# Six row-tile buffers for five, convolution stores and loads moved behind a countdown, and a paired inverse moved by two slots

## The chip, the cores and the metric

The kernel runs on one core of a Trainium2 chip. The metric is the device time of one execution in microseconds. Before the change the median of three runs is 1872.39 us (1871.93 to 1872.93).

## What is computed

The reference is the forward pass and all gradients of a layer with two branches on a layer norm of `A_q` (2048 rows of 1024). Branch A multiplies a long causal convolution, done by a Fourier transform of length 4096 per column, with the row; branch B is a gated MLP of width 3584. Cut to what matters:

```python
xn = _layernorm(x)                                     # x = A_q
# branch A
k_shift = sum(k_pad[:, t:t + S] * shift_k[:, ks - 1 - t] for t in range(ks))   # ks = 4
kv = k_shift * v
y = irfft2(rfft2(kv_pad) * rfft2(ssm_k_pad).T)[:S] + kv * ssm_D
a = xn * y
# branch B
gate, up = xn @ W_gate, xn @ W_up
gate = gate * (gate > 0)
b = (gate * up) @ W_down
out = x + a + b                                        # and the vjp of it for grad_out
```

The outputs are `out` and the gradients of `A_q`, `A_k`, `A_v`, `A_shift_k`, `A_ssm_k`, `A_ssm_D` and the three weights. All are bfloat16.

## The kernel before, in words

**Two branches on one TensorE.** Class `LnMlp` holds branch B's large products, class `ABranch` the convolution and its gradient. B's phases are generators that yield at the end of each piece of work with a number of nanoseconds. The main loop takes that number off a budget, and whenever the budget is used up it takes one *slot* of A: `ABranch.steps` (L577) runs through `slots` (L677) for eight groups of 128 columns. A slot has a tensor part `p` (a few small matmuls into PSUM tiles `ps_c`, evicted by ScalarE) and a vector part `d` (one VectorE step). It charges 1900 ns, or, once B is past its hidden phase (`dense`), 1250 ns when it has no tensor part.

**B's phases.** `hidden` (L1100) walks 14 blocks: seven column blocks of 512 for each half of the rows, eight row tiles a block. A row tile takes three products of eight 128x512 matmuls: `gate` (tile `ps_g`), `up` (`ps_u`) and `grad_row` (`ps_h`), all issued at L1041. ScalarE writes the ReLU of the gate into the row tile `ru` (L1149), VectorE the masked `up` (L1156) and their product `ht` (L1162); ScalarE copies `ps_h` to `gh` (L1284), and VectorE multiplies `ru` by it (L1285). `ht` is stored to `h_d` (L1167), `ru` to `ug_d` (L1290), both two ticks after they are asked for (`defer`, `tick`). `ru` comes from the pool `e2` (five buffers, L839; the later phases take their output tiles `wo` and `wi` from it), `ht` and `gh` from `e1`. The last four rows of a block are taken in another order, gate gate up gate gate up grad up up grad grad grad (`last_rows`); from there to the block's end `hold` is set. At the end of the last block, and before the next phase, `g_nat`, the natural rows of `grad_out`, are loaded into tiles that were `xnT` and `goT`.

`grad_down` computes the gradient of `W_down`, `grad_in` those of `W_gate` and `W_up`, in products of sixteen matmuls over the row tiles (`gemm16`, L1376). The first and the last turn of the former and the first of the latter are done by `four` (L1392): four PSUM banks at a time, so that the row tiles are needed more slowly, or come free sooner; meanwhile `cap` is 2 instead of 3, so a slot of A takes at most two pairs of banks. `xn_nat` rows take the tiles of `g_nat` when the last `four` of `grad_down` is done with them. Then follow `out_phase` (L1540) and `grad_x` (L1672), for which A's memory is released: weights `wd` (L1501) and the transposed row tiles `hT` (L1506) go there.

**PSUM.** One pool of eight banks, `b_ps`, serves both branches. A's slot takes up to six of them.

**A's transfers.** Everything is issued on SP's queue: A's loads (L99), A's stores (L107), B's loads, slabs (L1358) and stores. While `strict` is set, each engine's instructions stay in program order, so what SP waits for holds up all that is behind it. Stores are issued where the code calls `store` (L105). Loads are put into `queue` by `fetch` and `later`; after each slot `steps` issues one of them (L609) unless `hold` is set, and `need` (L262) issues those that are about to be read, hold or no hold. `load_filter` issues the first half of the filter rows `hn` and puts the second, `load_rest`, at the end of the queue. Most of A's tiles have one buffer, so a load waits until the tile's last reader is done.

**A's time-domain tiles.** `ttile` (L256) gives tiles of 19 rows x 128 from three tags: `gkv` and `gk` in tag ts0, `gks` and `gh` in ts1, `gv` and `yt` in ts2. Rows 16 to 18 hold the halo of `gks`.

**The paired inverse.** `inv_a_pair` gives four jobs `inv[0..3]`; `inv[1]` reads spectra that the complex product `cmul(H, K, ...)` has just written, and is the tensor part of the slot right behind `halo` (L747). `tables` (L140) fills the sine tables before the first slot.

Of the kernel before, what the change touches and what calls it, by code (L numbers as in the profile page):

```python
# [11 lines left out]
BF16 = mybir.dt.bfloat16  # L12
F32 = mybir.dt.float32
I32 = mybir.dt.int32
# [3 lines left out]
P = 128  # L18
# [27 lines left out]
NB1 = 32  # L46


class ABranch:
# [5 lines left out]
    def __init__(self, tc, pri, S, D, k, v, g, shift_k, ssm_k, ssm_D, xn_d, y_d, sk_d, gks_d, gh_d, out_gk,  # L55
                 out_gv, out_gsD):
        assert S == 2048 and D % P == 0
        self.tc, self.nc, self.pri = tc, tc.nc, pri
        self.S, self.D, self.NG = S, D, D // P
        self.k, self.v, self.g, self.shift_k, self.ssm_k, self.ssm_D = k, v, g, shift_k, ssm_k, ssm_D  # L60
        self.xn_d, self.y_d, self.sk_d = xn_d, y_d, sk_d
        self.gks_d, self.gh_d, self.out_gk, self.out_gv, self.out_gsD = gks_d, gh_d, out_gk, out_gv, out_gsD
        self.pools, self.pin, self.dense, self.queue = [], False, False, []
        self.cap = 3

    def pool(self, name, bufs, **kw):
        p = self.tc.alloc_tile_pool(name=name, bufs=bufs, **kw)
# [35 lines left out]
            self.pri.pin(ins)  # L103

    def store(self, out, in_):  # L105
        self.pri.late()
        self.pri.pin(self.nc.sync.dma_start(out=out, in_=in_))  # L107

    def open(self):
        R = "right"  # L110
# [29 lines left out]
    def tables(self):  # L140
        nc, con, big, pri = self.nc, self.con, self.big, self.pri
# [40 lines left out]
        for ri in range(2):  # L182
            off = lin(b32, -1024.0, 1024.0 * (1 + ri) + 2048.0, "offF%d" % ri)
            q = big.tile([P, NB1, NB1], I32, name="qF", tag="big")
# [20 lines left out]
        q = big.tile([P, 3, 8, NB1], I32, name="qI", tag="big")  # L205
# [7 lines left out]

        kk = lin(b5, 4.0, 1.0, "kkB")
        ob = lin(b32, 32.0, 96.0, "obB")
        itB = con.tile([P, NB1], I32, name="itB")
        hold(nc.gpsimd.iota(itB[:], pattern=[[1, NB1]], base=0, channel_multiplier=0))
        V.tensor_scalar(out=itB[:], in0=itB[:], scalar1=kk[:], scalar2=ob[:], op0=ALU.mult, op1=ALU.add)
        V.tensor_single_scalar(out=itB[:], in_=itB[:], scalar=127, op=ALU.bitwise_and)
        trB = con.tile([P, NB1], F32, name="trB")  # L220
        nc.scalar.activation(out=trB[:], in_=itB[:], func=ACT.Sin, scale=TWO_PI / 128, bias=negpi[:])
        for h in range(2):
            m = lin(b64, (2 * h - 1) / 1024.0, (1 - h) / 1024.0, "mB%d" % h)
# [30 lines left out]
    HOME = dict(gkv=0, gks=1, gv=2, gk=0, yt=2, gh=1)  # L254

    def ttile(self, name):  # L256
        return self.ts.tile([P, 19, P], BF16, name=name, tag="ts%d" % self.HOME[name])

    def later(self, f, st):
        self.queue.append((f, st))  # L260

    def need(self, f, st):  # L262

        while (f, st) in self.queue:
            self.issue()

    def issue(self):
        f, st = self.queue.pop(0)
        f(st)

    def load_filter(self, st):
        hn = self.lng.tile([P, 19, P], BF16, name="hn", tag="hk")[:, 0:16, :].rearrange("p r c -> p (r c)")
        st["hn"] = hn.rearrange("p (h c n) -> p h c n", h=2, n=NB1)
        self.load_rows(st, 0)
        self.later(self.load_rest, st)

    def load_rows(self, st, h):
        hv = self.ssm_k[st["cg"]].rearrange("(h x c) (q n) -> x h q c n", h=2, x=2, n=NB1)
# [298 lines left out]
    def steps(self):  # L577

        sk_t = self.shift_rows()
        self.pin = True
        yield 10000
        self.load(self.sk_d, sk_t[:])
        yield 25000
        self.sts = [dict(gi=gi, cg=slice(gi * P, (gi + 1) * P)) for gi in range(self.NG)]
        st = self.sts[0]
        self.load_filter(st)
        self.issue()
        yield 3400  # L590
        self.load_g(st)
        yield 3400
        self.load_v(st)
        yield 3400
        self.load_taps(st)
        yield 6800
        self.load_xn(st)
        self.pin = False
        self.pri.strict = True
        self.open_arena()  # L600
        for st in self.sts:
            for p, d in self.slots(st, st["gi"]):
                *more, last = self.parts(p)
                for fs in more:
                    self.tensor(fs)
                    yield self.DENSE[0]
                self.tensor(last)
                self.run(d)
                if self.queue and not self.hold():  # L609
                    self.issue()  # L610
                yield self.DENSE[p is None] if self.dense else self.SLOT

    def begin(self, st):
        st["ksh"] = self.lng.tile([P, 16, P], BF16, name="ksh")
# [62 lines left out]
    def slots(self, st, gi):  # L677
# [68 lines left out]
        yield [], lambda: self.halo(st)  # L746
        ia, inv = self.inv_a_pair()  # L747
        q = self.cmul(K, G, True, G, 1)
        yield inv[1], q
        for _ in range(4):  # L750
            yield None, q
        q = self.cmul(H, K, False, K, 1)
        cross, gk = [inv[0], None], None
        if not last:
# [71 lines left out]
class LnMlp:  # L826
# [7 lines left out]
    def open_left(self):  # L834
        tc = self.tc
        self.per = tc.alloc_tile_pool(name="b_per", bufs=1, side="left")
        self.actp = tc.alloc_tile_pool(name="b_act", bufs=1, side="left")
        self.w2 = tc.alloc_tile_pool(name="b_w2", bufs=1, side="left")
        self.e2 = tc.alloc_tile_pool(name="b_e2", bufs=5, side="left")  # L839
        self.e1 = tc.alloc_tile_pool(name="b_e1", bufs=5, side="left")  # L840
        self.ps = tc.alloc_tile_pool(name="b_ps", bufs=8, space=bass.MemoryType.PSUM)
        self.ln_x, self.xn, self.todo, self.hold = [], [], [[]], False
        self.rstd = self.per.tile([P, self.ST], F32, name="rstd")
        self.ident = self.per.tile([P, P], BF16, name="ident")
        make_identity(self.nc, self.ident[:])
# [859 lines left out]
@with_exitstack  # L1705
def kernel(
    ctx: ExitStack,
    tc: tile.TileContext,
    A_q: bass.AP,
    A_k: bass.AP,  # L1710
    A_v: bass.AP,
    A_shift_k: bass.AP,
    A_ssm_k: bass.AP,
    A_ssm_D: bass.AP,
    B_x: bass.AP,
    B_W_gate: bass.AP,
    B_W_up: bass.AP,
    B_W_down: bass.AP,
    grad_out: bass.AP,
    out_0: bass.AP,  # L1720
    out_1: bass.AP,
    out_2: bass.AP,
    out_3: bass.AP,
    out_4: bass.AP,
    out_5: bass.AP,
    out_6: bass.AP,
    out_7: bass.AP,
    out_8: bass.AP,
    out_9: bass.AP,
):  # L1730
    _, S, D = A_q.shape
    F = B_W_gate.shape[1]
    assert S % 256 == 0 and D == 1024 and F % 256 == 0
    x, g = A_q[0], grad_out[0]
    dram = ctx.enter_context(tc.tile_pool(name="dram", bufs=1, space=bass.MemoryType.DRAM))
    xn_d = dram.tile([S, D], BF16, name="xn_d")
    y_d = dram.tile([S, D], BF16, name="y_d")
    h_d = dram.tile([S, F], BF16, name="h_d")
    ug_d = dram.tile([S, 2, F], BF16, name="ug_d")

    gks_d = dram.tile([D // P, P, S], BF16, name="gks_d")
    gh_d = dram.tile([D // P, P, S], BF16, name="gh_d")
    sk_d = dram.tile([D // P * 4, P], BF16, name="sk_d")

    pri = Pri(tc)
    b = LnMlp(tc, pri, S, D, F)
    a = ABranch(tc, pri, S, D, A_k[0], A_v[0], g, A_shift_k, A_ssm_k, A_ssm_D, xn_d, y_d, sk_d[:], gks_d, gh_d, out_2[0],
                out_3[0], out_6)
    b.open_left()
    a.open()  # L1750
    a.identA, a.bank, b.branch = b.ident, b.ps_tile, a
    a.hold = lambda: b.hold
    pri.now()
    load = lambda i: b.ln_load(x, a.lnx, i)
    load(0)
    load(1)
    b.first_root()
    first = [b.col_block(B_W_gate, 0, "wg", 0)]
    first.append(b.col_block(B_W_up, 0, "wu", 1, lambda: load(2)))
    load(3)  # L1760
    first.append(b.row_block_T(B_W_down, 0, "wdT", 2, lambda: load(4)))
    goT = [b.load_T(g, i, "goT", 8 + i) for i in range(2)]
    load(5)
    goT += [b.load_T(g, i, "goT", 8 + i) for i in range(2, 4)]
    a.load_shift()
    ln = b.layer_norm(xn_d, a.tmp, "tmp", a.sm)
    def mlp():
        yield False, b.hidden(first, goT, load, ln, a.tables, B_W_gate, B_W_up, B_W_down, g, xn_d, h_d, ug_d)
        yield True, b.grad_down(xn_d, ug_d, h_d, out_9)
        yield True, b.grad_in(ug_d, out_7, out_8)  # L1770

    a_steps, left = a.steps(), A_START
    if True:
        for a.dense, phase in mlp():
            for ns in phase:
                left -= ns
                while a_steps is not None and left <= 0:
                    d = next(a_steps, None)
                    if d is None:
                        a.close()  # L1780
                        a_steps = None
                        pri.strict = False
                        b.open_right(B_W_down)
                    else:
                        left += d
    b.close_left()
    b.out_phase(x, xn_d, y_d, h_d, B_W_gate, B_W_up, out_0[0])
    b.grad_x(x, g, xn_d, y_d, h_d, ug_d, B_W_down, out_0[0], out_1[0],
             (A_k[0], gks_d, gh_d, out_4, out_5))
# [30 lines left out]
```

## Time and profile before

| what | us |
|---|---|
| median of three runs | 1872.39 |
| the profiled execution | 1871.87 |
| its span, first to last instruction | 1869.7 |
| TensorE busy / idle | 1853.3 / 16.4 |
| VectorE, ScalarE, POOL busy | 1113.7, 646.3, 19.4 |
| mean granted TensorE clock | 0.998 |

In the waits by engine, ScalarE's ReLU at L1149 waits for `ug_d<-ru`, the store of a row tile, five times, 19.5 us in all and 8.0 at most. SP's longest wait for A is that of a store at L107 for ScalarE's `yt`, 9.8 us; its loads at L99 wait 30.6 us in nine places for `ps_c` matmuls. The moved instructions of A in the table of DMA issues: `hn` 32 issues of 128 KB, 4.7 us median to landing; `vt`, `xt`, `kp` 16 each of 256 KB, 4.1 to 4.3 us; `gv`, `yt`, `gk` 16 each of 256 KB, 6.7, 4.5 and 5.0 us; `gks` and `gh` eight each of 512 KB, 2.7 and 7.2 us.

How to read it: TensorE's busy time is nearly the whole span, so a part matters if it ends an idle stretch of TensorE, or makes one. An idle stretch shows as a number ahead of a group or of a piece of the timeline, with the instruction or DMA that ended it. The granted clock of a window is a share of full speed. On SP's timeline "SPq" lines are issues: start, time the issue took, line, what is moved.

### The profile page before, as it was taken

What the parts mean: (1) busy time and instruction counts of PE and PEld (TensorE: products, weight loads), DVE (VectorE), ACT (ScalarE), POOL (GpSimd) and SP (SyncE); (2) the same over time, 40 slices, a digit from 0 to 9 for tenths busy, and PEclk for the clock granted to TensorE, in tenths of its full rate; (3) what the DMA queues carried; (4) which work ended last, traced back from release to release, by engine and by line L of the source; (5) the groups of instructions that cost most, each with busy time, mean ns of one, the idle gap of its engine ahead of it and who ended that gap; (6) DMA issues with size and microseconds to landing.
All of it is one profiled execution on the core that took longest, in us unless ns stands there. A gap on an engine that the chain in (4) does not pass through costs nothing.

```text
span 1869.7 us, 32060 instructions
## 1 busy us (share of the span) xinstructions
PE 1853.3 (99%) x13061; PEld 846.7 (45%) x13061; DVE 1113.7 (60%) x1635; ACT 646.3 (35%) x1215; POOL 19.4 (1%) x51
## 2 busy tenths in 40 slices
PE   9999999899999999999999999999999999999999
PEld 4444444444444444444444444444444544444444
DVE  6656897697789668485785677720222222466652
ACT  5744445445444454544545554331000000111100
POOL 1000000000000000000000000000000000000000
PEclk9999999999999999999999999999999999999999
DMA  9897678868868767467556454469999857799973
GB/s 265 244 224 183 151 199 202 213 163 185 188 151 204 216 160 189 125 168 205 164 144 160 118 161 118 144 178 274 261 215 257 206 135 174 179 210 203 209 154 74
DMA packets 748132, 344.65 MB, mean 184 GB/s; under 512 B 576088, under 2 KB 715344, under 8 KB 747984
## 3 DMA queue, kind: packets, MB, share of 16 engines
q1 hardware_dynamic: 736848, 320.31, 71.0%
q10 hardware_dynamic: 9504, 17.04, 3.0%
q0 software_dynamic: 1632, 5.24, 0.8%
q8 instruction: 102, 1.67, 0.4%
q14 instruction: 46, 0.38, 0.1%
HBM read 143.79 MB, written 103.83 MB: 132 GB/s over the span
## 4 chain that ended last, share of the span: by engine, by line
PE 95%; DVE 2%; DMA 2%; ACT 1%; issue 0%; SPq 0%; ACTq 0%; DVEq 0%
PE ps_x L1672 21%; PE ps_w L1376 20%; PE ps_o L1540 10%; PE ps_g L1041 10%; PE ps_u L1041 10%; PE ps_h L1041 9%; PE ps_d L1376 9%; PE ps_c L83 4%; PE ps_d L1392 1%; DVE ru L1156 0%; DMA g_nat<-in_grad_out_dram 0%; DVE arena L334 0%; PE ps_r L1574 0%; PE ps_w L1392 0%; DMA xn_nat<-xn_d 0%
## 5 line engine op out<-in xcount | busy, mean ns | idle before, releaser
L1376 PE MATMUL ps_w<-ugs,xn_nat 128*128 128x512 bf16 x1728 | 381.3, 379 | 0.0
L87 ACT CAST arena<-ps_c 128x512 bf16<-128x512 f32 x576 | 293.9, 610 | 109.2 <-PE ps_c L83 108.9
L1041 PEld LDWEIGHTS <-xnT 128*128 128x128 bf16 x1792 | 172.5, 98 | 215.7 <-issue 12.6
L334 DVE STREAM_TRANSPOSE arena<-arena 128x1024 f32<-128x1024 f32 x96 | 179.5, 1931 | 137.0 <-ACT arena L87 118.0
L1376 PEld LDWEIGHTS <-xn_nat 128*128 128x128 bf16 x1728 | 165.3, 98 | 201.4 <-issue 7.3
L1041 PE MATMUL ps_g<-wg,xnT 128*128 128x512 bf16 x896 | 206.5, 381 | 5.6 <-ACT ru L1149 4.9
L1041 PE MATMUL ps_u<-wu,xnT 128*128 128x512 bf16 x896 | 206.0, 379 | 0.0
L1041 PE MATMUL ps_h<-wdT,goT 128*128 128x512 bf16 x896 | 204.8, 379 | 0.0
L1672 PE MATMUL ps_x<-wgT,ggT 128*128 128x512 bf16 x896 | 198.6, 379 | 0.0
L1672 PE MATMUL ps_x<-wuT,guT 128*128 128x512 bf16 x896 | 198.6, 379 | 0.0
L1690 ACT ACTIVATE w<-xn,m 128x512 f32<-128x512 bf16 x32 | 24.4, 808 | 480.3 <-DVE m L1683 366.7
L1540 PE MATMUL ps_o<-wd,hT 128*128 128x512 bf16 (+1 forms) x896 | 187.6, 372 | 0.0
L1376 PE MATMUL ps_d<-g_nat,hs 128*128 128x512 bf16 x768 | 170.1, 379 | 0.0
L1672 PEld LDWEIGHTS <-guT 128*128 128x128 bf16 x896 | 87.7, 98 | 105.7
L1672 PEld LDWEIGHTS <-ggT 128*128 128x128 bf16 x896 | 87.7, 98 | 105.5
L1041 PEld LDWEIGHTS <-goT 128*128 128x128 bf16 x896 | 86.0, 98 | 103.9 <-issue 2.9
L1540 PEld LDWEIGHTS <-hT 128*128 128x128 bf16 x896 | 87.7, 98 | 99.9
L1284 ACT CAST gh<-ps_h 128x512 bf16<-128x512 f32 x112 | 66.5, 595 | 178.3 <-PE ps_h L1041 177.2
L1379 ACT CAST wi<-ps_w 128x512 bf16<-128x512 f32 x108 | 64.6, 598 | 181.5 <-PE ps_w L1376 145.2
L1156 DVE SCALAR_TENSOR_TENSOR ru<-ru,ps_u 128x512 bf16<-128x512 bf16 x112 | 76.5, 683 | 81.6 <-PE ps_u L1041 56.0
L1532 DVE TENSOR_TENSOR ya<-ya,xe 128x1024 bf16<-128x1024 bf16 x16 | 11.1, 692 | 173.6 <-DMA xe<-xn_d 173.6
L91 DVE TENSOR_TENSOR t<-arena 128x2048 bf16<-128x2048 bf16 x96 | 113.9, 1219 | 0.4
(145 smaller groups left out, 1393.6 us busy)
## 6 DMA issues: line engine op xcount, KB each, us to landing
ugs<-ug_d SPq DMA_DIRECT2D x112, 256.0 KB, 5.0
ug_d<-ru SPq DMA_DIRECT2D x110, 256.0 KB, 3.0
wg<-in_B_W_gate_dram SPq DMA_DIRECT2D x56, 256.0 KB, 3.6
wu<-in_B_W_up_dram SPq DMA_DIRECT2D x56, 256.0 KB, 3.2
hs<-h_d SPq DMA_DIRECT2D x56, 256.0 KB, 4.2
out_dram<-wi SPq DMA_DIRECT2D x56, 256.0 KB, 2.5
h_d<-ht SPq DMA_DIRECT2D x108, 128.0 KB, 3.3
gt<-in_grad_out_dram SPq DMA_DIRECT2D x32, 256.0 KB, 4.5
```

The lines of the kernel that those rows point to most:

```text
L83: self.pri.pin(self.nc.tensor.matmul(out, lhsT=lhsT, rhs=rhs, start=start, stop=stop))
L87: self.pri.pin(self.nc.scalar.copy(out=out, in_=in_))
L91: self.pri.pin(self.nc.vector.tensor_tensor(out=out, in0=in0, in1=in1, op=op))
L334: self.pri.pin(self.nc.vector.transpose(out=df[:, c0:c0 + 32, :], in_=sf[:, c0:c0 + 32, :]))
L1041: self.pri.pin(self.nc.tensor.matmul(ps[:], lhsT=xT[:, kt * P:(kt + 1) * P], rhs=w(kt), start=(kt == 0), stop=(kt == self.DT - 1)), always ...
L1156: return self.pri.pin(nc.vector.scalar_tensor_tensor(out=ru[s][:, 1, :], in0=ru[s][:, 0, :], scalar=0.0, in1=ps[:], op0=ALU.is_gt, op1=ALU ...
L1284: self.pri.pin(nc.scalar.copy(out=gh[:], in_=ps[:]))
L1376: self.pri.pin(self.nc.tensor.matmul(ps[:], lhsT=lhsT(st), rhs=rhs(st), start=(st == 0), stop=(st == self.ST - 1)))
L1379: self.pri.pin(self.nc.scalar.copy(out=out, in_=ps[:]))
L1540: nc.tensor.matmul(ps, lhsT=hT[:, kt, :], rhs=self.wd[:, kt, oc], start=(kt == 0), stop=(kt == self.FT - 1))
L1672: nc.tensor.matmul(ps, lhsT=T[:, kt, :], rhs=W[:, kt, oc], start=(i == 0), stop=(i == n - 1))
L1690: nc.scalar.activation(out=w[:, oc], in_=xn[:, oc], func=ACT.Identity, scale=m[:, 7:8], bias=m[:, 6:7])
```

## The change

It does six things.

- The pool `e2` has six buffers instead of five.
- `store` no longer issues: it puts the transfer in a list `out` with a countdown of 3. After each slot's vector part `stores` takes one off every countdown and issues, in order, those at 0. A store thus goes out at the end of the third slot from where it was called. At A's end the rest is issued.
- `later` gives each queued load the same countdown; the queue's first is issued when it has reached 0. The countdown runs on in the slot that would have issued the load, so it goes out two slots after that at the earliest. `load_rest` goes to the front of the queue without a countdown.
- `a.hold` is also true while `cap` is 2, that is during `four`. `need` overrides both.
- `inv[1]` stands in the third of its five slots instead of the first; the number of slots is the same.
- `ttile` gives 16 rows unless the tag is ts1, and two small tiles of the sine tables, `itB` and `trB`, take the buffers of tags ts2 and ts1.

```diff
-        self.cap = 3
+        self.cap, self.out = 3, []
...
     def store(self, out, in_):
-        self.pri.late()
-        self.pri.pin(self.nc.sync.dma_start(out=out, in_=in_))
+        self.out.append([self.WAIT, out, in_])
+
+    def stores(self):
+        for o in self.out:
+            o[0] -= 1
+        while self.out and self.out[0][0] <= 0:
+            _, out, in_ = self.out.pop(0)
+            self.pri.late()
+            self.pri.pin(self.nc.sync.dma_start(out=out, in_=in_))
+
+    WAIT = 3
...
-        itB = con.tile([P, NB1], I32, name="itB")
+        itB = self.ts.tile([P, NB1], I32, name="itB", tag="ts2")
...
-        trB = con.tile([P, NB1], F32, name="trB")
+        trB = self.ts.tile([P, NB1], F32, name="trB", tag="ts1")
...
     def ttile(self, name):
-        return self.ts.tile([P, 19, P], BF16, name=name, tag="ts%d" % self.HOME[name])
+        h = self.HOME[name]
+        return self.ts.tile([P, 19 if h == 1 else 16, P], BF16, name=name, tag="ts%d" % h)
 
     def later(self, f, st):
-        self.queue.append((f, st))
+        self.queue.append([f, st, self.WAIT])
 
     def need(self, f, st):
 
-        while (f, st) in self.queue:
+        while any(e[0] == f and e[1] is st for e in self.queue):
             self.issue()
 
     def issue(self):
-        f, st = self.queue.pop(0)
+        f, st, _ = self.queue.pop(0)
         f(st)
...
         self.load_rows(st, 0)
-        self.later(self.load_rest, st)
+        self.queue.insert(0, [self.load_rest, st, 0])
...
                 self.run(d)
-                if self.queue and not self.hold():
+                self.stores()
+                for e in self.queue:
+                    e[2] -= 1
+                if self.queue and self.queue[0][2] <= 0 and not self.hold():
                     self.issue()
                 yield self.DENSE[p is None] if self.dense else self.SLOT
+        while self.out:
+            self.stores()
...
         q = self.cmul(K, G, True, G, 1)
+        yield None, q
+        yield None, q
         yield inv[1], q
-        for _ in range(4):
-            yield None, q
+        yield None, q
+        yield None, q
...
-        self.e2 = tc.alloc_tile_pool(name="b_e2", bufs=5, side="left")
+        self.e2 = tc.alloc_tile_pool(name="b_e2", bufs=6, side="left")
...
-    a.hold = lambda: b.hold
+    a.hold = lambda: b.hold or a.cap == 2
```

## The prediction

> **What bounds the kernel now.** I read the page's busy times first, then TensorE's groups by shape with the idle time ahead of them, then windows and timelines around the largest gaps.
>
> ```profile
> PE 1853.3 (99%) x13061; PEld 846.7 (45%) x13061; DVE 1113.7 (60%) x1635; ACT 646.3 (35%) x1215; POOL 19.4 (1%) x51
> ```
> TensorE works 1853.3 of 1869.7 us. No matmul is added or removed, so nothing can be won but the 16.4 us of idle time and what a lowered clock costs. The groups say who ended the idle time:
>
> ```profile
> L1041 PE MATMUL ps_g<-wg,xnT 128*128 128x512 bf16 x896 | 206.5, 381 | 5.6 <-ACT ru L1149 4.9 <-DVE xnT L1085 0.3 <-DVE ru L1156 0.2
> L1392 PE MATMUL ps_d<-g_nat,hs 128*128 128x512 bf16 x128 | 30.6, 391 | 1.8 <-DMA g_nat<-in_grad_out_dram 1.8
> L83 PE MATMUL ps_c<-arena,IA 32*64 32x256 bf16 x1024 | 30.0, 274 | 1.2 <-DVE arena L91 1.2
> L1392 PE MATMUL ps_w<-ugs,xn_nat 128*128 128x512 bf16 x64 | 15.0, 380 | 0.7 <-DMA xn_nat<-xn_d 0.7
> ```
> That is 5.6 + 1.8 + 1.2 + 0.7 = 9.3 us; the rest is the start (3.7 with 0.3 of ps_g's), the tail after the last matmul (3.2) and one wait of the convolution for ScalarE (0.7). The clock dips at the first two places:
>
> ```profile
> 345.00:350.00 5.00, 2.88 (x58) 1.39 (x57) 1.11 (x2) 0.00 (x0) 0.00 (x0) 1.00 0.87 241
> 350.00:355.00 5.00, 2.20 (x6) 0.83 (x6) 1.22 (x3) 2.85 (x6) 0.00 (x0) 0.74 1.03 289
> 355.00:360.00 5.00, 5.00 (x52) 2.15 (x51) 0.76 (x1) 3.35 (x8) 0.00 (x0) 0.92 0.95 247
> ...
> 650.00:655.00 5.00, 3.71 (x17) 1.04 (x17) 0.95 (x1) 2.35 (x5) 0.00 (x0) 0.78 1.02 337
> 655.00:660.00 5.00, 5.00 (x22) 2.11 (x21) 5.00 (x4) 1.33 (x3) 0.00 (x0) 0.88 0.99 218
> ```
> Column three from the end is the granted clock: (0.26 + 0.08) x 5 = 1.7 us lost at 350, (0.22 + 0.12) x 5 = 1.7 at 650.
>
> **The 4.9 us stall at 347.9.** The PE, ScalarE and SP timelines:
>
> ```profile
> 345.98 1.90 PE L1041 MATMUL ps_u<-wu,xnT 128*128 128x512 bf16 x8
> 352.80 5.08 PE L1041 MATMUL ps_g<-wg,xnT 128*128 128x512 bf16 x16 [4.92 <-ACT ru L1149]
> ```
> ```profile
> 343.58 0.60 ACT L1149 ACTIVATE ru<-ps_g 128x512 bf16<-128x512 f32 x1 [0.33 <-PE ps_g L1041]
> 352.15 0.60 ACT L1149 ACTIVATE ru<-ps_g 128x512 bf16<-128x512 f32 x1 [7.97 <-DMA ug_d<-ru]
> ```
> ```profile
> 339.07 1.47 SPq L1290 DMA_DIRECT2D ug_d<-ru  x1
> 340.59 2.17 SPq L99 DMA_DIRECT2D hn<-in_A_ssm_k_dram  x2
> 342.86 2.00 SPq L107 DMA_DIRECT2D out_dram<-gk  x2
> 344.96 1.32 SPq L1167 DMA_DIRECT2D h_d<-ht  x1
> 346.38 1.07 SPq L107 DMA_DIRECT2D out_dram<-gh  x1
> 347.55 0.36 SPq L107 DMA_DIRECT2D gh_d<-gh  x1
> 348.00 0.52 SPq L1167 DMA_DIRECT2D h_d<-ht  x1
> 348.61 0.59 SPq L1290 DMA_DIRECT2D ug_d<-ru  x1
> ```
> The ReLU of row 5 has no free ru buffer: it waits for the store issued at 348.61 (landed 352.07), whose data VectorE had finished at 330.7. SP was simply behind, back to back since 323.9. Queued behind the ReLU are six convolution evictions, and with them, the second ps_g and a ps_u all eight PSUM banks are full. The previous row's store, issued at 339.07, had landed at 342.96.
>
> **The change, part by part.**
>
> *Sixth buffer.* Rows take buffers in turn, so row 5 gets the one free since 342.96, ahead of its ps_g's end at 345.2. This removes 4.92 + 1.7 = **6.6 us**. What is late next: row 6's ReLU, which without the stall is due near 345.2 + 0.85 (ps_c) + 1.73 (ps_u) + 1.73 (ps_g) = 349.6, and needs the store that landed at 352.07. That is 2.4 us of ScalarE, while PE can fill the seventh ps_g, four ps_c banks and a ps_u before it lacks a bank, about 1.7 + 0.6 + 1.7 = 4.0 us: nothing. Nor does the stream catch on weights: SP issues the next wg at 357.45 to 359.0, landed 363.4, and the matmuls due at 370.5 move to 363.9, the last of the four tiles to 365.1. If SP ran 2 us later this would cost 0.3 us.
>
> *Stores three slots later* (counted down at the end of each slot, from 3). No instruction is added. At 347 the gh pair (1.07 + 0.36 and gaps, 1.6 us) falls behind row 0's store, which helps it. The larger effect is at the end of the hidden phase:
>
> ```profile
> 642.82 1.34 SPq L107 DMA_DIRECT2D y_d<-yt  x2
> 644.25 1.35 SPq L1290 DMA_DIRECT2D ug_d<-ru  x1
> 645.65 2.96 SPq L1071 DMA_DIRECT2D g_nat<-in_grad_out_dram  x4
> ```
> Its last issue ended at 640.0; SP stands to 642.8 for ScalarE's yt, then spends 1.34 us on it; behind it wait a ug_d store whose data was ready at 641.2 and the last four g_nat loads. Three slots later yt is behind the g_nat loads and the eight hs loads. The loads go about 645.65 - 641.75 = 3.9 us sooner; the last landed 652.81, its matmul was due at 652.85 - 1.84 = 651.0, so 2 us are to spare. Gain 1.84 us and the clock's 1.7: **3.5 us**. Bounds: 0, if bandwidth rather than issue sets the landing; 3.5, all there is.
> [...]
>
> *Loads later, and none amid the four-bank products* (an entry waits until the end of the second slot after the one that would have issued it, and load_rest now goes first). At 859.1 the gt and sD loads hold SP for 2.2 us ahead of the eight xn_nat loads, whose landings ended PE waits of 0.28 and 0.37 us at 870. They now come after 878: **0.65 us** (bounds 0 and 0.65). On the other side the held loads must still be in time. The tightest: the filter rows hn, issued at 653.9 to 662.8, now after 660.2; they took 4.7 us to land, and are read at 685.2, so some 15 us remain. vt of group 3 may fall into the hold from 573 to 595; xt went at 597.7 after that hold, so vt lands about 603, for a product due near 614. The kp memset on POOL moves with its load, and nothing else stands on POOL then. Cost 0; if the cover were gone, one wait would cost SP's issue of the four hn loads (5.34 and 2.1 us at 653.9 and 660.7), a landing of 4.7, and 1.7 of clock: 13.9 us.
> [...]
>
> *Paired inverse two slots later.* PE waits for VectorE's last products at 250 (0.45 + 0.28), 417 (0.17) and 576 (0.29). VectorE ended them at 251.4; two slots are near 4 us, so PE comes at 254.7. Gain **1.2 us** (bounds 0 and 1.2). Its four evictions fall beside two gates, 4 + 2 banks of eight.
>
> *Storage* (16 rows for 19, sine tables in reused tiles, and the end of the convolution): a few small VectorE, ScalarE and POOL steps before 100 us may wait for each other; PE shows no idle from 50 to 250, its banks cover some 4 us. Cost 0, at most 2. After the convolution's end the last gk and gh stores stand just ahead of the wd loads: the fourth landed at 1287.4, due at 1286.03 + 21 x 0.216 = 1290.6, so 3.2 us are spare: 0, at most 2.
>
> Sum: 6.6 + 3.5 + 0.65 + 1.2 = 12.0 us. Profiled time 1871.87 (span 1869.7 and 2.2 around it) becomes 1859.9; the median stands 0.5 above that execution, so **1860.4 us**.
>
> **Rivals.**
> (a) *The g_nat wait stays*, because at 650 to 655 DMA moves 337 GB/s, the most of the five windows above: 12.0 - 3.5, 1863.9 us. Against it, SP's idle 2.7 us. Chance 0.12.
> (b) *The change doesn't reach the 347 stall*: SP is 18 us behind there, and three slots are 6; if the added buffer goes elsewhere in the rotation the wait stays: 12.0 - 6.6, 1867.0. Against it, the landing at 342.96. Chance 0.08.
> (c) *One held load comes due while not landed*, the price above, 13.9: 1874.3. Chance 0.08.
> (d) The other side, the same mechanism at its second place, where the hold and the countdown add up to a load that `need` issues at once and PE's in-order queue stands: from two such waits the kernel is slower, 1860.4 + 2 x 13.9 = 1888.2. For it: the first two hn issues after the hold took SP 5.3 us, where a pair mostly takes 2; against: 10 us and more of margin at the tightest places. Chance 0.06.
> The forecast has 0.66.
>
> **How the numbers follow.** Low end: all idle time but start and tail, with both dips, is 16.4 - 6.9 + 3.4 = 12.9, and 0.5 for the runs' spread: 1859.0. High end 1867.2 takes in (b), and (a) with the small costs (0.3 for wg and 2 of storage). About 0.2%, 3.7 us, is what a measurement of this kernel tells from no change; faster is 0.66 + 0.12 + 0.08 = 0.86, same (c) 0.08, slower (d) 0.06.
>
> **What would show it.** Right: no gap above 1 us in ps_g's group; no ScalarE wait for ug_d above 3 us; clock 1.00 in every window but the last; ps_d at L1392 without a DMA wait, g_nat issued ahead of y_d; L83's IA group at 0.0 idle. Wrong: a wait of ps_c for hn, of VectorE for vt, kp or xt ahead of a PE gap, or ps_o waiting for wd.

## The result, and the profile after

Six executions of each kernel: 1859.48 us (median, 1858.79 to 1860.24) after the change, 1872.66 us (1871.23 to 1874.43) before it. The ratio is 0.9929 (95% interval 0.9916 to 0.9942): 13.2 us less. The forecast was 1860.4, faster. One execution of a run below, `e4_stores_at_once`, took 6731.48 us, against some 1862 in its others, and is left out of its figures.

The profiled execution took 1858.79 us with a span of 1857.0. The busy times and TensorE's groups by shape, as on the page of before:

```profile
PE 1850.1 (100%) x13061; PEld 845.7 (46%) x13061; DVE 1114.1 (60%) x1635; ACT 645.7 (35%) x1215; POOL 19.4 (1%) x51
```
```profile
L1058 PE MATMUL ps_g<-wg,xnT 128*128 128x512 bf16 x896 | 205.0, 379 | 0.6 <-DVE xnT L1102 0.3 <-DVE ru L1173 0.2
L1409 PE MATMUL ps_d<-g_nat,hs 128*128 128x512 bf16 x128 | 28.6, 379 | 0.0
L83 PE MATMUL ps_c<-arena,IA 32*64 32x256 bf16 x1024 | 29.4, 274 | 0.0
L1409 PE MATMUL ps_w<-ugs,xn_nat 128*128 128x512 bf16 x64 | 14.5, 379 | 0.0
```
(L1058, L1166, L1301, L1307 and L1409 are the old L1041, L1149, L1284, L1290 and L1392.) The four idle times of before, 5.6, 1.8, 1.2 and 0.7 us, are 0.6, 0.0, 0.0 and 0.0; of the 0.6, 0.3 is a wait at the start and 0.2 one for VectorE's `ru` at 484, which the kernel before has too. TensorE's idle time fell from 16.4 to 6.9 us, its busy time by 3.2: the `ps_g` and `ps_d` matmuls last 379 ns each, against means of 381 and 391 before, where the granted clock fell to 0.74 and 0.78 in the windows of the prediction. The windows, with the granted clock third from the end:

```profile
345.00:350.00 5.00, 4.76 (x44) 2.18 (x35) 2.87 (x6) 4.34 (x10) 0.00 (x0) 1.00 0.87 201
350.00:355.00 5.00, 5.00 (x54) 2.23 (x52) 2.25 (x4) 2.58 (x6) 0.00 (x0) 1.00 1.00 309
640.00:645.00 5.00, 5.00 (x67) 2.07 (x66) 3.76 (x3) 3.55 (x7) 0.00 (x0) 1.00 1.00 324
```
Both dips are gone: the clock is 1.00 in these windows, and in those from 645 to 660. The `g_nat` matmuls that waited now stand in the third of these windows, and the DMA engines move 324 GB/s there without a wait.

Where the time came from is best read by stages, cut where the first matmul of each kind starts (worked out from the trace, us):

| kernel | start, to the first ps_h | hidden, to the first ps_d | first `four` | rest of grad_down | grad_in | out_phase, grad_x | span |
|---|---|---|---|---|---|---|---|
| before | 24.20 | 617.08 | 18.93 | 200.47 | 425.36 | 583.70 | 1869.7 |
| after | 24.45 | 609.12 | 14.93 | 200.47 | 424.34 | 583.72 | 1857.0 |
| difference | +0.25 | -7.96 | -4.00 | 0.00 | -1.02 | +0.02 | -12.7 |

The stages that the change was not to touch agree to 0.02 us, so in these some tenths can be read. The start varies by up to 0.84 us between the runs below, whatever the kernel, and the hidden stage by 1.4 us between two executions whose code up to its end is the same (609.12 here and 610.51 in `e6` below): a difference there is read from the single waits.

### The profile page after: what moved, and what is told of

Read it like the earlier page. It is cut to its first block, busy times and chain, and to the rows that moved or that the text cites. A ratio compares the mean times of both kernels' runs of the same rounds, so it can differ in the third digit from the quotient of the medians.

```text
span 1857.0 us, 32063 instructions
## 1 busy us (share of the span) xinstructions
PE 1850.1 (100%) x13061; PEld 845.7 (46%) x13061; DVE 1114.1 (60%) x1635; ACT 645.7 (35%) x1215; POOL 19.4 (1%) x51
## 4 chain that ended last, share of the span: by engine, by line
PE 98%; SPq 1%; DMA 1%; DVE 0%; ACT 0%; issue 0%; ACTq 0%
PE ps_x L1689 21%; PE ps_w L1393 20%; PE ps_h L1058 10%; PE ps_o L1557 10%; PE ps_u L1058 10%; PE ps_g L1058 10%; PE ps_d L1393 9%; PE ps_c L83 4%; PE ps_d L1409 2%; PE ps_w L1409 1%; SPq L1076 1%; DMA goT<-in_grad_out_dram 0%; PE ps_r L1591 0%; DMA wg<-in_B_W_gate_dram 0%; DVE arena L344 0%
## 5 line engine op out<-in xcount | busy, mean ns | idle before, releaser
L1058 PEld LDWEIGHTS <-xnT 128*128 128x128 bf16 x1792 | 172.0, 98 | 209.7 <-issue 5.7
L1058 PE MATMUL ps_u<-wu,xnT 128*128 128x512 bf16 x896 | 206.1, 379 | 0.1
L1058 PE MATMUL ps_g<-wg,xnT 128*128 128x512 bf16 x896 | 205.0, 379 | 0.6 <-DVE xnT L1102 0.3
L1058 PE MATMUL ps_h<-wdT,goT 128*128 128x512 bf16 x896 | 204.9, 379 | 0.6 <-DMA goT<-in_grad_out_dram 0.6
L1058 PEld LDWEIGHTS <-goT 128*128 128x128 bf16 x896 | 85.7, 98 | 105.1 <-issue 2.9
L1301 ACT CAST gh<-ps_h 128x512 bf16<-128x512 f32 x112 | 66.4, 594 | 184.4 <-PE ps_h L1058 175.0
```

The lines of the kernel that those rows point to most:

```text
L1058: self.pri.pin(self.nc.tensor.matmul(ps[:], lhsT=xT[:, kt * P:(kt + 1) * P], rhs=w(kt), start=(kt == 0), stop=(kt == self.DT - 1)), always ...
L1301: self.pri.pin(nc.scalar.copy(out=gh[:], in_=ps[:]))
```

## The experiments

Theory: the four terms of the sum are four separate causes. Rivals: the store order alone clears the stall at 347, or the buffer alone does; bandwidth and not issue sets the `g_nat` landings; the held loads do nothing, or are close to coming late.

### The buffer alone, and the stores alone

`e1_buffer_alone` is the kernel before with the sixth buffer (and the smaller tiles that make room for it, not shown here):

```diff
-        self.e2 = tc.alloc_tile_pool(name="b_e2", bufs=5, side="left")
+        self.e2 = tc.alloc_tile_pool(name="b_e2", bufs=6, side="left")
```

> The kernel before with the sixth row-tile buffer alone (and the smaller tiles that make room for it); stores, loads and inverse as before. Theory (the sixth buffer removes the 4.9 us stall at 347.9 by itself, with its 1.7 us of lowered clock): no TensorE gap above 1 us near 347, the four g_nat waits near 643 stay (1.8 us and a clock dip), the waits on VectorE ahead of the paired inverse stay (1.2 us); time 6.6 us below before, about 1866. Rival (the later stores of the convolution cure the stall, since SP is 18 us behind there): the stall stays at 4 to 5 us, time as before.

Measured: 1865.02 us, ratio 0.9963 (0.9948 to 0.9978). The hidden stage is 610.58, 6.50 us less; TensorE has no gap at 347. The waits for `g_nat` stay. TensorE's timeline in this run (start, length, and the idle time ahead in brackets):

```profile
641.53 0.82 PE L1393 MATMUL ps_d<-g_nat,hs 128*128 128x512 bf16 x3
643.69 0.38 PE L1393 MATMUL ps_d<-g_nat,hs 128*128 128x512 bf16 x1 [1.34 <-DMA g_nat<-in_grad_out_dram]
644.60 0.81 PE L1393 MATMUL ps_d<-g_nat,hs 128*128 128x512 bf16 x3 [0.53 <-DMA g_nat<-in_grad_out_dram]
645.78 0.38 PE L1393 MATMUL ps_d<-g_nat,hs 128*128 128x512 bf16 x1 [0.38 <-DMA g_nat<-in_grad_out_dram]
646.44 0.38 PE L1393 MATMUL ps_d<-g_nat,hs 128*128 128x512 bf16 x1 [0.29 <-DMA g_nat<-in_grad_out_dram]
```
That is 2.5 us of waits, 0.7 more than in the profile of before, yet the clock stayed at 1.00 here, and `four` took 18.10 us, less than before's 18.93. Of the four executions of `e1`, two took 1863.39 and 1864.20 us (this one) at a mean clock of 1.000, and two 1865.85 and 1866.54 at 0.999, as one dip would make: those of before last 3.41 us at a granted clock of 0.50, so 1.7 us are lost of some 1862. By this estimate the same kernel has a dip in some executions and none in others; where those two had theirs isn't on record.

`e3_stores_alone` is the kernel before with `store`, `stores` and their two calls alone.

```diff
     def store(self, out, in_):
-        self.pri.late()
-        self.pri.pin(self.nc.sync.dma_start(out=out, in_=in_))
+        self.out.append([self.WAIT, out, in_])
...
                 self.run(d)
+                self.stores()
```

> The kernel before with the countdown of 3 on the convolution's stores alone; five buffers, loads and inverse as before. Theory: the g_nat waits at the end of the hidden phase go (1.84 us and 1.7 of clock), and the stall at 347 shrinks to 1.5 to 3.5 us: 5 to 8 us below before, about 1865 to 1867. Rival (g_nat is held by bandwidth, not by SP standing behind yt): g_nat waits stay near 1.8 us, at most 3 us below before.

Measured: 1865.29 us, ratio 0.9963 (0.9949 to 0.9977). `four` takes 14.93 us, 4.0 less: the `g_nat` waits are gone without the buffer. The hidden stage is 616.96, only 0.12 less, because the stall is still there in the profiled execution, in two pieces. TensorE's timeline of it, then ScalarE's:

```profile
346.17 0.41 PE L83 MATMUL ps_c<-arena,FW 64*32 64x256 bf16 x15 [0.85 <-ACT gh L1296]
346.67 1.89 PE L1053 MATMUL ps_u<-wu,xnT 128*128 128x512 bf16 x8
351.93 4.44 PE L1053 MATMUL ps_g<-wg,xnT 128*128 128x512 bf16 x12 [3.38 <-ACT ru L1161]
```
```profile
345.53 0.58 ACT L1296 CAST gh<-ps_h 128x512 bf16<-128x512 f32 x1 [3.37 <-DMA h_d<-ht]
351.28 0.60 ACT L1161 ACTIVATE ru<-ps_g 128x512 bf16<-128x512 f32 x1 [4.67 <-DMA ug_d<-ru]
```
The ReLU waits 4.67 us for a `ru` store instead of 7.97, but ScalarE first waits 3.37 us for an `h_d` store, which it doesn't in the kernel before: `gh` and `ht` come from another pool, `e1`. With the clock's dip (0.71 in the window 350 to 355) the two pieces cost what the one had. This execution, 1866.79 us, is the slowest of five, though. The others took 1864.47 to 1865.50, and three of them had a mean clock of 1.000, against 0.999 here, so no dip; by their times about 1.5 us depends on it.

### The change without one of the two

`e2_five_buffers` is the changed kernel with `bufs=5`.

> The changed kernel with five buffers again. Theory (row 5 then waits for row 0's store, which the changed order issues at 345.45 instead of 348.61; with the 3.5 us that this store took to land, ScalarE goes on at 348.9, and TensorE some 0.7 us later, against full banks at about 347.9): a TensorE gap of 1.5 to 2 us near 347, with or without a clock dip, so 1.7 to 3.5 us above the changed kernel, 1861 to 1863. Rival (only the buffer counts, the order of the queue does nothing there): the gap is 4.9 us again and the time 6.6 above the changed kernel, 1866.

Measured: 1862.88 us, ratio 0.9952 (0.9937 to 0.9967), 3.4 us more than the changed kernel. `four` is 14.93; the hidden stage is 4.39 longer than after the change. The stall is back at 2.79 us, with a dip:

```profile
345.52 1.89 PE L1058 MATMUL ps_u<-wu,xnT 128*128 128x512 bf16 x8
350.20 4.13 PE L1058 MATMUL ps_g<-wg,xnT 128*128 128x512 bf16 x12 [2.79 <-ACT ru L1166]
```
So at 347 the buffer carries the gain; the other order on SP shortens the stall without removing it. The gap is larger than the 1.5 to 2 us expected since the store that the ReLU waits for, issued at 345.23, took 4.3 us to land. All four executions have a mean clock of 0.999.

`e4_stores_at_once` and its repeat `e11_stores_again` are the changed kernel with stores issued where they are called.

```diff
-        self.out.append([self.WAIT, out, in_])
+        self.pri.late()
+        self.pri.pin(self.nc.sync.dma_start(out=out, in_=in_))
```

> The changed kernel with the stores issued where they are called, as before. Theory: no stall at 347 (the sixth buffer covers it), but SP stands for yt ahead of the last g_nat loads again: TensorE waits for g_nat of 1.5 to 2 us near 640 and a clock dip, 3 to 4 us above the changed kernel, about 1863. Rival (the loads held out of the four-bank products, or the buffer, made room for g_nat): no g_nat wait, same time as the changed kernel.

> The changed kernel with the stores issued at once, profiled a second time. Theory: g_nat waits of about 2.5 us again, with a dip (19.5 us in the first four-bank stage) or without (17.9). Rival (this order never dips): 17.9 us.

Measured: 1861.81 us (median of three), ratio 0.9946 (0.993 to 0.9963), and 1861.37 in one run; 2 us more than the changed kernel, where 3 to 4 with a dip were expected. No stall at 347 (hidden 609.21 and 609.17). `four` takes 17.85 and 17.58 us, with three waits for `g_nat` of 2.45 and 1.99 us in all, and no dip (a mean clock of 1.000 in both). TensorE's waits in `e4`, then SP's issues in it and in the changed kernel:

```profile
642.36 0.38 PE L1410 MATMUL ps_d<-g_nat,hs 128*128 128x512 bf16 x1 [0.85 <-DMA g_nat<-in_grad_out_dram]
643.38 1.02 PE L1410 MATMUL ps_d<-g_nat,hs 128*128 128x512 bf16 x4 [0.64 <-DMA g_nat<-in_grad_out_dram]
645.36 0.38 PE L1410 MATMUL ps_d<-g_nat,hs 128*128 128x512 bf16 x1 [0.95 <-DMA g_nat<-in_grad_out_dram]
```
```profile
634.88 1.34 SPq L107 DMA_DIRECT2D y_d<-yt  x2
636.31 1.35 SPq L1308 DMA_DIRECT2D ug_d<-ru  x1
637.71 2.93 SPq L1089 DMA_DIRECT2D g_nat<-in_grad_out_dram  x4
640.70 5.00 SPq L1376 DMA_DIRECT2D hs<-h_d  x8
```
```profile
634.07 2.65 SPq L1088 DMA_DIRECT2D g_nat<-in_grad_out_dram  x4
636.77 5.39 SPq L1375 DMA_DIRECT2D hs<-h_d  x8
642.59 0.54 SPq L1307 DMA_DIRECT2D ug_d<-ru  x1
643.34 2.58 SPq L114 DMA_DIRECT2D y_d<-yt  x2
```
Counted from the first ps_d matmul (633.34 and 633.57), the four loads start 4.37 us behind it in the one and 0.50 in the other; before the change it was 4.37 too (645.65 less 641.28). The last of them landed 11.96 us behind it against 8.2, 11.53 before. Every run with `y_d` ahead of the loads has the waits, every run with it behind has none.

### Loads and the paired inverse

`e5_loads_back` is the changed kernel with a countdown of 0 and the old `hold` (`load_rest` still goes first); `e6_loads_amid_four` undoes the `hold` alone.

```diff
     def later(self, f, st):
-        self.queue.append([f, st, self.WAIT])
+        self.queue.append([f, st, 0])
...
-    a.hold = lambda: b.hold or a.cap == 2
+    a.hold = lambda: b.hold
```

> The changed kernel with both changes to the loads undone: no countdown on loads, and loads issued amid the four-bank products again (the stores' countdown, the sixth buffer and the inverse stay). Theory: only the two waits for xn_nat near 860 come back, 0.65 us of idle time and about 1 us in the stage, since gt stands ahead of the xn_nat loads again; 1860 to 1861. Rival 1 (the countdown on loads also unblocks SP in the hidden phase): a gap above 1 us near 347 comes back, 3 us or more slower. Rival 2 (nothing hangs on the loads): no gap at 860, same time.

> The changed kernel with the countdown on loads kept, but loads let out amid the four-bank products. Theory (the hold, not the countdown, moves gt behind the xn_nat loads): the waits for xn_nat near 860 are back, 0.5 to 1 us in that stage; all else as in the changed kernel. Rival (the countdown of two more slots alone carries gt past them): no wait there.

Measured: `e5` 1859.51 us, ratio 0.9927 (0.991 to 0.9943), no different in the median from the changed kernel; but its `grad_in` takes 425.26 us, 0.9 more. SP's issues in it, and behind them what TensorE shows:

```profile
846.61 1.32 SPq L99 DMA_DIRECT2D gt<-in_grad_out_dram  x2
847.98 0.83 SPq L99 DMA_DIRECT2D sD<-in_A_ssm_D_dram  x1
848.85 4.50 SPq L1088 DMA_DIRECT2D xn_nat<-xn_d  x8
```
```profile
857.68 0.39 PE L1409 MATMUL ps_w<-ugs,xn_nat 128*128 128x512 bf16 x1 [0.27 <-DMA xn_nat<-xn_d]
858.33 0.39 PE L1409 MATMUL ps_w<-ugs,xn_nat 128*128 128x512 bf16 x1 [0.26 <-DMA xn_nat<-xn_d]
```
In the changed kernel SP issues 13 `xn_nat` loads in a row from 838.09, and no wait is left there. In `e6` (1859.79, one run) `grad_in` is 424.24 and there is no wait of that size: the countdown alone carries `gt` past the `xn_nat` loads, and the `hold` during `four` is not needed for it, as the rival had it. `e6`'s hidden stage is 1.4 us longer than after the change, 1.0 of it at one TensorE wait of 1.18 us at 344.8 for ScalarE's `gh`, the `e1` pool again. The `hold` that it undoes has no effect at that time, so this may be chance; one run can't say.

`e7_inverse_back` is the changed kernel with the inverse where it was.

```diff
-        yield None, q
-        yield None, q
         yield inv[1], q
-        yield None, q
-        yield None, q
+        for _ in range(4):
+            yield None, q
```

> The changed kernel with the paired inverse in the first of its five slots again. Theory: TensorE waits for VectorE ahead of it at about 250, 410 and 570 again, 1.2 us of idle time in all, and 1.9 to 2.3 us of stage time (each gap also costs the pipeline's refill); about 1861 to 1862. Rival (the new place of the inverse took its idle time elsewhere, beside the gates): the waits come back but the end moves by less than 0.5 us.

Measured: 1860.08 us (one run), which by itself lies within the changed kernel's 1858.79 to 1860.24. The four waits are back (0.45, 0.29, 0.20 and 0.28 us); the first two:

```profile
250.76 0.32 PE L83 MATMUL ps_c<-arena,IA 32*64 32x256 bf16 x8 [0.45 <-DVE arena L91]
251.36 0.53 PE L83 MATMUL ps_c<-arena,IA 32*64 32x256 bf16 x24 [0.29 <-DVE arena L91]
```
At 250, 411 and 571 the hidden stage falls behind by 1.0, 0.4 and 0.5 us. In all it is 1.70 longer, as the wait for `gh` near 345 was 0.2 shorter; the later stages agree to 0.1 us.

### How far the loads can be moved

The changed kernel with a countdown for loads of 26 slots (`e8_loads_26`) and of 16 (`e12_loads_16`) instead of 3, to price rivals (c) and (d):

```diff
-        self.queue.append([f, st, self.WAIT])
+        self.queue.append([f, st, 26])
```

> The changed kernel with a countdown of 26 on the loads instead of 3; stores at 3. It prices the fourth rival of the prediction, a held load that comes due. From its queueing to its use vt has some 22 slots, kp 28, hn some 30. Theory: vt (and what is queued ahead of it) is now issued by need in the slot ahead of its product, once in each of seven groups; VectorE waits for the landing, 4 to 7 us each, and TensorE, whose kvt product stands two slots later, 2 to 6 us each: 12 to 40 us slower than the changed kernel, with gaps ahead of ps_c<-kp. Rival (A's slots have enough room for a late load): VectorE waits, TensorE does not, less than 3 us slower.

> The changed kernel with a countdown of 16 slots on the loads, between 3 (no cost seen) and 26 (51 us). Theory (a load costs nothing as long as its countdown ends before need calls for it; by the count of slots vt is called for 22 after it is queued, kp and hn about 30): outside the hidden phase nothing is lost, and in it, where the hold of 11 slots comes on top, one or two of vt, kp and hn are called early, 0 to 14 us in all. Rival (the cost grows with every slot of delay, since the issue collides with more of B's loads): about 13/23 of the 51 us, 29 us, spread over all stages.

Measured: 1911.07 us with 26, 51.6 more than the changed kernel, and 1868.38 with 16, 8.9 more (one run each). With 26, loads that `need` issues at once hold TensorE up at 206, 302, 387, 635, 716 and 1150, directly or through VectorE. Its timeline at two of these:

```profile
301.58 0.30 PE L83 MATMUL ps_c<-arena,IA 32*64 32x256 bf16 x4
312.03 0.64 PE L83 MATMUL ps_c<-kp,R 32*64 32x512 bf16 x4 [10.15 <-DVE kp L91]
...
395.61 0.58 PE L83 MATMUL ps_c<-hn,R 32*64 32x512 bf16 x1 [8.11 <-DMA hn<-in_A_ssm_k_dram]
398.40 0.64 PE L83 MATMUL ps_c<-hn,R 32*64 32x512 bf16 x3 [2.21 <-DMA hn<-in_A_ssm_k_dram]
```
In the first, VectorE's `kp` waited 8.16 us for `vt`, issued at 304.88. The second is what the prediction described: SP issued the four `hn` loads at 388.74, when TensorE already stood there, took 5.85 us over them, and the last was there 3.8 us after that. Each came with 10.2 us at half clock (granted 0.67, 0.50 and 0.81 in the three windows of 5 us from 305, and 0.70, 0.50 and 0.78 from 390), more than half of it while TensorE stood; what was left of it cost 2.4 us at 301 (to 316.9, from 312.0) and 1.9 at 387 (to 402.2, from 398.4). So a load due while not landed cost 12.6 and 12.2 us. The run as a whole missed the 12 to 40 us expected of it, waits of 2 to 6 us in up to seven groups: there were fewer places, two with over 10 us, and a lowered clock at each, which the expectation had left out.

With 16, inside the 0 to 14 us expected, only one load of A stops TensorE by itself (`hn` behind 205.75, 1.5 us); the rest is spread: 2.9 us of waits for `wg` at 365 to 369 with a dip (the run's mean clock is 0.999), 0.7 and 0.9 us for `kp`, 1.2 for VectorE's `ru`. The `wg` wait is no A load at all: SP issued the four `hn` loads in two pairs, at 347.5 and 352.9, where in the changed kernel they went at 334.0 and 339.4, and `wg` behind them at 362.4 instead of 356.5. The margin of the held loads is thus not used up by a countdown of 3; the first waits come between 3 and 16 slots, and those of 10 us beyond 16.

### The kernel before, twice more

`e9_before_again` and `e10_before_third` are the kernel before, unchanged, to see whether its dips are a matter of luck; the time in question is that of the first `four`, 18.93 us in the first profile.

> The kernel before, unchanged, profiled again, to see whether the lowered clock after the four g_nat waits belongs to them. Two runs with larger g_nat waits (2.5 us) showed none. [...] Rival (the dip is a fixed consequence of these four waits): 18.9 us with a dip again.

> As the run before it: the unchanged kernel a third time. Theory: 18.9 us with a dip or some 17.2 without it. Rival: 18.9 us with a dip.

Measured: 1875.23 and 1873.82 us. The stall at 347 is 4.73 and 4.76 us, with the dip; the `g_nat` waits are 2.66 and 2.86 us. `e9` has twice the dip of the first profile there, (0.17 + 0.50) x 5 = 3.4 us lost against 1.7; `e10` has the same length of `four`. The windows of `e9_before_again`:

```profile
650.00:655.00 5.00, 2.43 (x14) 0.60 (x13) 0.30 (x1) 1.23 (x4) 0.00 (x0) 0.83 0.90 297
655.00:660.00 5.00, 5.00 (x19) 1.65 (x12) 4.46 (x3) 2.21 (x4) 0.00 (x0) 0.50 1.05 271
```
`four` takes 21.3 us in both, 6.4 more than after the change, against 4.0 by the first profile; neither expectation had this. Both have a mean clock of 0.997; of the eight executions of before that were timed beside `e1`, three have that, four 0.998 and one 0.999, by an estimate from the 1.7 us of one dip some three, two and one of them. In all three profiles of before the waits came with a dip; in the three with such waits but without the stall (`e1`, `e4`, `e11`) none did, but two other executions of `e1` show one somewhere. That the stall must come first is not shown.

## Why the prediction was right

The forecast's mechanisms held at all four places, each shown by doing or undoing it alone; one wait that the change itself made was not foreseen. The sizes:

| term | forecast | measured | by |
|---|---|---|---|
| sixth buffer, stall at 347.9 | 6.6 | 6.5 | `e1`, hidden stage |
| stores later, `g_nat` | 3.5 | 4.0; 6.4 in two more executions of before; 2.7 to 3.2 where no dip came | `e3`, `four`; `e9`, `e10`; `e1`, `e4`, `e11` |
| loads later, `xn_nat` | 0.65 | 0.9 to 1.0 | `e5`, and before less after |
| inverse later | 1.2 | 1.9 at its three places | `e7` |
| the new wait for `gh` | none | -0.6 | the profile after |
| sum | 12.0 | 12.7 in span, 13.2 in the median | |

**The terms that were too small.** The prediction took the waits as the profile states them. A matmul of 512 columns is shown 0.379 us long, while in an undisturbed run the next one starts 0.216 us after it. The idle time is counted from the end of the 0.379, so each gap behind such a matmul costs 0.163 more than its number: a wait of 0.447 us at 250 in before is 0.610 us more between starts. With four gaps each for `g_nat` and the inverse and two for `xn_nat`, that adds about 0.65, 0.65 and 0.33: 1.84 + 0.65 leave 1.5 of the 4.0 of `four` for the clock, where the dip's 3.41 us at 0.50 would make up to 1.7; 1.2 + 0.65 is near the 1.9 of the inverse (where most gaps stand behind shorter matmuls, so that 0.65 is rough); and 0.65 + 0.33 is the 1.0 of `grad_in`. That the sum came within 0.7 us all the same owes something to the new wait for `gh`, on the other side.

**The stall at 347.** What is late next was to be row 6's ReLU, by 2.4 us on ScalarE, at no cost to TensorE. ScalarE's timeline of the changed kernel:

```profile
344.64 0.58 ACT L1301 CAST gh<-ps_h 128x512 bf16<-128x512 f32 x1 [2.66 <-DMA h_d<-ht]
...
349.80 0.60 ACT L1166 ACTIVATE ru<-ps_g 128x512 bf16<-128x512 f32 x1 [0.66 <-DMA ug_d<-ru]
352.81 0.60 ACT L1166 ACTIVATE ru<-ps_g 128x512 bf16<-128x512 f32 x1 [2.42 <-DMA ug_d<-ru]
```
TensorE has no gap at the last two, so the cost was right. The 2.42 us are a coincidence, though: row 6 is the line above, with 0.66, since its store went out at 345.45 instead of 348.61, and the 2.42 are row 7's, for a store issued at 349.43. With the buffer alone (`e1`) row 6 waits 3.55, and TensorE has no gap either. What the prediction had not seen is the first line: ScalarE waits 2.66 us for an `h_d` store, which costs TensorE 0.24 us of idle in two gaps (0.58 between starts), and 1.18 us of idle in `e6`. It comes with the moved stores and not with the sixth buffer: `e2` and `e3`, with five buffers and the stores moved, have it (2.75 and 3.37 us), and no run with the stores issued where they are called does, with five buffers (before, `e9`, `e10`) or six (`e1`, `e4`, `e11`). Why the new order makes `gh` wait for that store no run shows.

**A remark that was half right.** The prediction had the later `gh` pair help at 347. Row 0's store does go out sooner, and with five buffers the ReLU waits 4.67 us in `e3` and 4.08 in `e2` instead of 7.97; but the new wait for `gh` takes part of that, and in `e3`'s profile the lowered clock the rest. No number of the sum rested on it.

**The stores at the end of the hidden phase.** The forecast had the loads go 3.9 us sooner with 2 us to spare: they went 3.87 us sooner, landed 3.3 us sooner, and TensorE waited for none. Issue and not bandwidth set the landing, and rival (a) falls: the same loads came in 3.3 us sooner by being issued sooner, with the DMA engines at 324 GB/s at 640 to 645, near the 337 that it was built on.

**The other rivals.** (b) falls by `e1`. (c) and (d) are a real mechanism at nearly the price given (13.9 forecast, 12.2 measured for `hn`; the 12.6 is another load, `vt`, through VectorE), but not at this distance: at 3 slots no wait for a held load is left, and at 16 the longest for one is 1.5 us.

**Parts costed at nothing.** The smaller tiles, the tables in reused tiles, the next weights and the end of the convolution cost no more than the start's scatter: TensorE shows no idle from 50 to 250, and `out_phase` with `grad_x` is 583.72 against 583.70. `gt` goes out at 860.43, behind the `xn_nat` loads as the forecast had it, if some 6 us sooner than its 878, which is 866 by the clock of the changed kernel.

**The median.** 13.2 us by the medians against 12.7 by the two spans. 0.4 of the difference lies outside the span (2.14 us around it before, 1.76 after). The dips differ from one execution of before to the next, so its median holds a mixture of them; the first profile, with two dips, is the middle case.

## What to carry to other kernels

On an engine that issues all transfers in program order, look at which issue stands to wait for its data, and at what is ready behind it: here a store that kept SP idle for 2.8 us before its turn held up loads worth 2.7 to 6.4 us, by whether the clock dipped, and it could go behind them, as nobody reads it soon. Look at once at what the new order does to the other buffers that the queue empties: here ScalarE came to wait for a store that it had not waited for, at 0.6 us. And price a gap between matmuls by their starts, not by the idle time shown (0.61 us for 0.45 here), and a scatter of gaps together with a lowered clock: here 1.84 us in four gaps came with 1.7 us lost that way in before, and 2.5 us in `e1` with none.

## What the runs showed of the hardware

**Small gaps came with half the clock in some runs and not in others.** The trace of before has two dips, each 3.41 us at a granted clock of 0.50, from 352.38 and from 652.76, with 1.00 between them and from the second to 1860. The 1.84 us of `g_nat` waits in before came with one such dip, the 2.66 in `e9` with twice as much, the 2.9 us of `wg` waits in `e12` with a dip too; the `g_nat` waits of 2.5 us in `e1`, 2.45 in `e4` and 1.99 in `e11` came with none. So the sum of the waits doesn't sort these cases, and what does no run here shows.

**A dip costs less where the engine stands anyway.** At the two waits of some 10 us in `e8` the clock was at half for 10.2 us, but only what lay beyond the end of the wait, 1.9 and 2.4 us after halving, was lost; at the 4.92 us stall of before the dip starts at 352.38 and the wait ends at 352.80, so by the same reckoning it is (3.41 - 0.42) / 2 = 1.5, not the 1.7 that the window's mean suggests.
